# Order of the sign and the high word in an on-chip float64 to float32 conversion

## The chip, the cores and the metric

The kernel runs on one core of a Trainium2 chip. The metric is the device time of one execution in microseconds (us). Times of several runs are told as their median.

## What is computed

Attention for 4 batches of 12 heads (448 rows of 64) with RMS-normalised queries and keys, then two feed-forward blocks on the 1792 rows of 768 features:

```python
q_n, k_n = rmsnorm(q, g_q), rmsnorm(k, g_k)
attn = softmax(q_n @ k_n.T / sqrt(64))
x = heads_joined(attn @ v)
h = x @ w_in                               # 768 -> 2048
x = maximum(0.01 * h, h) @ w_out           # 2048 -> 768
h = (x @ w1) * (x @ w2) @ w3               # 768 -> 1024 -> 1024
out = (h @ w_out2).astype(float32)         # 1024 -> 768
```

All inputs of the attention are float32. The weights of the two blocks come as float64 (each was a float32 array multiplied by a float64 scalar), so the kernel gets them as pairs of 32-bit words and makes float32 of them on the chip.

## The kernel before

The program is laid out in three parts. `attention_steps` (lines 403 to 422) walks the 48 heads; for each head it emits the values of the head two before, four transposes of the probabilities of the head before, four score blocks of this head and its loads. Between these steps a generator of matrix products is advanced: first `combine_weights` (lines 564 to 591), which multiplies w3 by the last weight matrix once, then `first_mlp` and `second_mlp` (lines 630 to 686) for the first two batches, first for batch 0 alone ("early", weights of two groups), then the rest. When the heads are done, `last_pair` (lines 923 to 975) does the last two batches; it reads weights that were kept in DRAM as float32.

Each product is three matmuls for each block of 128 rows, on a high and a low part of weights and data (`group`, lines 544 to 561). After each three matmuls `group` calls `pump` (lines 529 to 535), which takes one piece of the generator `Weights.work` (lines 517 to 527) as long as fewer than two tiles are ready beyond those taken. `take` (lines 537 to 542) draws all pieces that are still missing when a tile is needed. Pieces are emitted with a priority that lets a planner place them up to 100 places earlier. The planner orders the instructions of every engine by priority and by when it reckons them ready, and gives out the buffers of the pools.

A wide weight tile (128 partitions, 768 or 512 columns, two words each) is loaded to `w64` (pool `cv`, two buffers, L459). `to_float32` (lines 461 to 486) makes float32 of it in three pieces, in a result tile `raw` (pool `wp`, three buffers):

- ScalarE takes the high word as a float and scales it by 2^-112 into `raw` (L477, called the high pass here).
- POOL makes the sign: it multiplies the high word by 0, in place, so that only its sign bit stays (L478).
- VectorE shifts `raw` left by 3 and joins the sign by "or" (L480, the join).
- ScalarE scales the low word to an integer by 2^-29, in place (L483, the low pass).
- VectorE adds the low word to the joined one as integers (L485, the add).

`split` (lines 488 to 515) then stores `raw` to DRAM if it is wanted again (L502), copies it to a rounded high part `wh` on ScalarE (L510) and subtracts that to get the low part `wl`, mostly on POOL (L203 by the helper `subtract`). There are 80 wide tiles: 8 of the last matrix, 16 of w3, 16 of w_in, 24 of w_out, 16 of w1 and w2. Kept tiles come as finished parts.

On the same engines run the attention's steps: VectorE turns the scores into p with a row minimum (L287), ScalarE takes the exponential (L296), ScalarE and VectorE copy the transposed p into two parts (L101, L203), POOL splits queries and values (`copy` L105, `subtract` L203).

Of the kernel before, what the change touches and what calls it, by code (L numbers as in the profile page):

```python
# [8 lines left out]
F32 = mybir.dt.float32  # L9
F32R = mybir.dt.float32r  # L10
U32 = mybir.dt.uint32
AF = mybir.ActivationFunctionType
ALU = mybir.AluOpType
# [35 lines left out]
def attention_then_moe(  # L49
# [22 lines left out]
    nc = tc.nc  # L72
# [352 lines left out]
    class Weights:  # L425
# [35 lines left out]
        def to_float32(self, t):  # L461

            m = self.size(t)  # L470
            self.raw[t] = wp.tile([P, WT], F32, tag="raw", name="raw")
            words = self.words.pop(t)
            low, high = words[:, :m, 0], words[:, :m, 1]
            out = self.raw[t][:, :m]
            top = out.bitcast(U32)
            signed = high.bitcast(F32)
            nc.scalar.activation(out, signed, AF.Copy, scale=2.0**-112)  # L477
            nc.gpsimd.tensor_scalar(signed, signed, 0.0, 1.0, op0=ALU.mult, op1=ALU.mult)  # L478
            yield
            nc.vector.scalar_tensor_tensor(  # L480
                top, top, 3, high, op0=ALU.logical_shift_left, op1=ALU.bitwise_or
            )
            nc.scalar.activation(low, low, AF.Copy, scale=2.0**-29)  # L483
            yield
            nc.vector.tensor_tensor(top, top, low, op=ALU.add)  # L485
            yield
# [648 lines left out]
```

## Time and profile before

| | us |
|---|---|
| median of 3 runs | 1273.02 |
| lowest and highest | 1272.32 and 1289.95 |
| the profiled execution's own time | 1278.26 |
| its span, first to last instruction | 1276.5 |
| TensorE (PE) busy in the span | 1171.5 |
| VectorE (DVE) busy | 817.2 |
| ScalarE (ACT) busy | 689.7 |
| POOL (GpSimd) busy | 496.0 |

All durations come from the one profiled execution. In the rows, PE is TensorE's matmul, PEld its weight load, DVE VectorE, ACT ScalarE, POOL GpSimd, SP the engine that issues the DMAs; `w<-w` is a tile of words, and `raw` the result tile. "L480" is line 480 of the kernel. Idle time of an engine is put down to what released the next instruction, behind "<-".

### The profile page before, as it was taken

Reading aid. Unit: us, or ns where it says so; the run is one execution under the profiler, and the core shown is the slowest. Engines: PE = TensorE matmul, PEld = TensorE weight load, DVE = VectorE, ACT = ScalarE, POOL = GpSimd, SP = SyncE. Lnnn points to the kernel's source line nnn. Section 1 sums busy time; section 2 is a strip of 40 time slices with the busy share of each in tenths; the row PEclk is TensorE's granted clock in tenths of the full one; section 3 lists DMA queues with packets and bytes.
Section 4 is the critical chain, followed back from the end, with each engine's and each line's share of the span. In section 5 each row is a group of like instructions: output and inputs, shape, how many; then the busy total and the mean of one; then the engine's idle time right before and its main releaser. Section 6 shows DMA issues by size and latency. Waiting matters only on the chain.

```text
span 1276.5 us, 17374 instructions
## 1 busy us (share of the span) xinstructions
PE 1171.5 (92%) x5816; PEld 1016.1 (80%) x5816; DVE 817.2 (64%) x1461; ACT 689.7 (54%) x1365; POOL 496.0 (39%) x470
## 2 busy tenths in 40 slices
PE   2879888898789999988989999999999999899998
PEld 1447587786668899877778899998999999699997
DVE  5986775879987465774775455358446464964553
ACT  5666666787667456545655566435442434443431
POOL 5565646777756256656766435420000000000000
PEclk9979999999889999999989999999999999899999
DMA  7767656899799955563555234135212020211212
GB/s 220 201 202 208 172 134 200 280 301 294 241 310 283 264 172 161 160 183 114 160 173 165 77 109 172 52 120 160 67 44 78 27 83 25 75 50 62 63 42 95
DMA packets 105609, 191.48 MB, mean 150 GB/s; under 512 B 23376, under 2 KB 62256, under 8 KB 105520
## 3 DMA queue, kind: packets, MB, share of 16 engines
q1 hardware_dynamic: 105520, 190.37, 49.6%
q8 instruction: 46, 0.75, 0.3%
q14 instruction: 43, 0.35, 0.1%
HBM read 136.74 MB, written 43.03 MB: 141 GB/s over the span
## 4 chain that ended last, share of the span: by engine, by line
PE 59%; DVE 14%; DMA 12%; issue 6%; POOL 5%; ACT 2%; SPq 1%; POOLq 0%; DVEq 0%; ACTq 0%
PE ps_mm L552 21%; PE ps_o L552 12%; PE ps_b L552 9%; PE ps_c L552 4%; PE pt L327 3%; PE po L381 3%; DVE raw L480 3%; PE ps_a L552 2%; PE pw L552 2%; DVE raw L485 2%; DMA w<-w 1%; PE ps L283 1%; DVE p L287 1%; PE ps L284 1%; DMA w<-w_last 1%
## 5 line engine op out<-in xcount | busy, mean ns | idle before, releaser
L203 POOL TENSOR_TENSOR wl<-raw,wh 128x512 fp32r<-128x512 f32 (+1 forms) x76 | 124.6, 1641 | 103.0 <-ACT wh L510 99.0
L296 ACT ACTIVATE p<-p,low 112x448 f32<-112x448 f32 x192 | 127.1, 663 | 55.3 <-DVE p L287 54.9
L203 DVE TENSOR_TENSOR ptl<-pt,pth 112x448 fp32r<-112x448 f32 x160 | 96.8, 617 | 80.2 <-ACT pth L101 78.0
L287 DVE TENSOR_SCALAR_CACHE_REDUCE p<-ps,rs 112x448 f32<-112x448 f32 x192 | 125.0, 676 | 35.2 <-PE pt L327 19.4
L552 PE MATMUL ps_mm<-xh,wh 128*128 128x448 f32 x384 | 142.8, 372 | 3.5 <-DMA wh<-kept_first_mlp_h 3.3
L552 PE MATMUL ps_mm<-xh,wl 128*128 128x448 f32 x384 | 142.5, 372 | 0.3 <-POOL wl L203 0.3
L552 PE MATMUL ps_mm<-xl,wh 128*128 128x448 f32 x384 | 142.7, 372 | 0.0
L327 PE MATMUL pt<-ident,p 112*112 112x112 f32 x768 | 115.2, 271 | 29.2 <-DVE ptl L203 20.5
L327 PEld LDWEIGHTS pt<-ident,p 112*112 112x112 f32 x768 | 88.3, 139 | 65.1 <-DVE ptl L203 28.4
L480 DVE SCALAR_TENSOR_TENSOR raw<-raw,w 128x768 uint32<-128x768 uint32 (+1 forms) x80 | 89.8, 1122 | 69.4 <-POOL w L478 69.2
L101 ACT ACTIVATE pth<-pt 112x448 fp32r<-112x448 f32 (+1 forms) x176 | 91.6, 534 | 49.5 <-PE pt L327 40.0
L552 PE MATMUL ps_mm<-gh,wh 128*128 128x448 f32 x288 | 107.5, 376 | 4.5 <-DVE acc L628 1.9
L283 PE MATMUL ps<-ks,qh 128*112 128x448 f32 x192 | 78.7, 413 | 32.0 <-DVE p L287 20.4
L552 PE MATMUL ps_mm<-gl,wh 128*128 128x448 f32 x288 | 106.8, 372 | 0.1
L552 PE MATMUL ps_mm<-gh,wl 128*128 128x448 f32 x288 | 106.7, 373 | 0.0
L552 PE MATMUL ps_o<-gl,wh 128*128 128x448 f32 x288 | 104.9, 365 | 0.0
L483 ACT ACTIVATE w<-w 128x768 uint32<-128x768 uint32 (+1 forms) x80 | 63.0, 788 | 74.0 <-DMA w<-w_out 25.5
L552 PE MATMUL ps_o<-gh,wl 128*128 128x448 f32 x288 | 102.5, 365 | 0.0
L552 PE MATMUL ps_o<-gh,wh 128*128 128x448 f32 x288 | 99.2, 365 | 0.8 <-DVE s L965 0.8
L477 ACT ACTIVATE raw<-w 128x768 f32<-128x768 f32 (+1 forms) x80 | 62.9, 787 | 61.5 <-POOL wl L203 22.4
L478 POOL TENSOR_SCALAR w<-w 128x768 f32<-128x768 f32 (+1 forms) x80 | 66.9, 836 | 69.3 <-ACT raw L477 59.1
L485 DVE CUSTOM_DVE_ANT_0 raw<-w,raw 128x1536 uint16<-128x1536 uint16 (+1 forms) x80 | 89.7, 1122 | 1.6
(140 smaller groups left out, 2926.7 us busy)
## 6 DMA issues: line engine op xcount, KB each, us to landing
w<-w_in SPq DMA_DIRECT2D x16, 768.0 KB, 6.2
w<-w_out SPq DMA_DIRECT2D x24, 512.0 KB, 5.3
w<-w SPq DMA_DIRECT2D x16, 768.0 KB, 4.9
qk_sb<-qk SPq DMA_DIRECT2D x48, 224.0 KB, 4.3
qt_sb<-qt SPq DMA_DIRECT2D x96, 112.0 KB, 3.6
w<-w3t SPq DMA_DIRECT2D x16, 512.0 KB, 4.8
w<-w_last SPq DMA_DIRECT2D x8, 768.0 KB, 7.1
kept_first_mlp<-raw SPq DMA_DIRECT2D x16, 384.0 KB, 4.1
```

Of the source, the lines that this page charges most:

```text
L101: nc.scalar.activation(out, x, AF.Copy)
L203: e.tensor_tensor(out, x, y.bitcast(F32), op=ALU.subtract)
L283: nc.tensor.matmul(ps, h["qh"][:, q], h["ks"], start=True, stop=False)
L287: nc.vector.tensor_scalar(p, ps, h["scale"][:, c : c + 1], None, op0=ALU.mult, op1=ALU.min, accum_out=low,)
L296: exps[i] = nc.scalar.activation(p, p, AF.Exp, bias=low, scale=-1.0, accum_out=h["sum"][:, c : c + 1])
L327: nc.tensor.transpose(pt[:, c * CP : (c + 1) * CP], h["p"][c][:, kc * CP : (kc + 1) * CP], ident[:CP, :CP],)
L477: nc.scalar.activation(out, signed, AF.Copy, scale=2.0**-112)
L478: nc.gpsimd.tensor_scalar(signed, signed, 0.0, 1.0, op0=ALU.mult, op1=ALU.mult)
L480: nc.vector.scalar_tensor_tensor(top, top, 3, high, op0=ALU.logical_shift_left, op1=ALU.bitwise_or)
L483: nc.scalar.activation(low, low, AF.Copy, scale=2.0**-29)
L485: nc.vector.tensor_tensor(top, top, low, op=ALU.add)
L552: nc.tensor.matmul(ps[:, :n], a, x, start=begin, stop=end, skip_group_check=on)
```

## The change

POOL makes the sign first, and writes it into the result tile. ScalarE scales the low word in the same piece. In a second piece ScalarE scales the high word in place. In a third piece VectorE shifts the high word, joins it with the sign and writes the result tile. The add is a fourth piece.

```diff
@@ -473,14 +473,15 @@
             low, high = words[:, :m, 0], words[:, :m, 1]
             out = self.raw[t][:, :m]
             top = out.bitcast(U32)
-            signed = high.bitcast(F32)
-            nc.scalar.activation(out, signed, AF.Copy, scale=2.0**-112)
-            nc.gpsimd.tensor_scalar(signed, signed, 0.0, 1.0, op0=ALU.mult, op1=ALU.mult)
+            h = high.bitcast(F32)
+            nc.gpsimd.tensor_scalar(out, h, 0.0, 1.0, op0=ALU.mult, op1=ALU.mult)
+            nc.scalar.activation(low, low, AF.Copy, scale=2.0**-29)
+            yield
+            nc.scalar.activation(h, h, AF.Copy, scale=2.0**-112)
             yield
             nc.vector.scalar_tensor_tensor(
-                top, top, 3, high, op0=ALU.logical_shift_left, op1=ALU.bitwise_or
+                top, high, 3, top, op0=ALU.logical_shift_left, op1=ALU.bitwise_or
             )
-            nc.scalar.activation(low, low, AF.Copy, scale=2.0**-29)
             yield
             nc.vector.tensor_tensor(top, top, low, op=ALU.add)
             yield
```

## Rows read from the trace of the kernel before

**Rows 1.** The page: the chain that ended last, share of the span by engine.

```profile
PE 59%; DVE 14%; DMA 12%; issue 6%; POOL 5%; ACT 2%; SPq 1%; POOLq 0%; DVEq 0%; ACTq 0%
```

**Rows 2.** Windows: length, PE, PEld, DVE, ACT, POOL busy us, granted clock, DMA share, GB/s.

```profile
0.00:100.00 100.00, 62.24 (x225) 37.67 (x226) 78.08 (x153) 62.81 (x120) 60.01 (x58) 0.90 0.73 208
100.00:700.00 600.00, 543.00 (x2798) 464.60 (x2797) 425.75 (x775) 378.59 (x794) 368.59 (x355) 0.97 0.70 210
700.00:850.00 150.00, 149.88 (x789) 136.38 (x789) 68.59 (x130) 78.69 (x156) 64.21 (x57) 1.00 0.30 97
850.00:1276.50 426.50, 416.42 (x2009) 377.41 (x2007) 244.73 (x404) 169.58 (x297) 3.19 (x3) 0.99 0.23 71
```

**Rows 3.** The chain by line, shares of the stretches 135:250, 250:400 and 520:700.

```profile
by line: issue 17.8%; DMA w<-w_in 12.6%; DMA w<-w3t 6.9%; PE pw L552 5.1%; POOL wl L203 5.1%; PE po L381 4.0%; DVE raw L485 3.7%; POOL w L478 3.5%; POOL ql L203 3.4%; POOL qh L105 3.2%; DMA kt_sb<-kt 2.9%; PE pt L327 2.7%; DMA wc<-wo 2.6%; 
...
by line: PE ps_mm L552 11.2%; DVE raw L480 9.1%; DVE p L287 6.0%; issue 5.8%; DVE ptl L203 5.4%; DMA rk<-rs 4.6%; DMA rk_sb<-rk 4.5%; DMA wh<-kept_first_mlp_h 4.4%; DVE raw L485 4.1%; DMA v_sb<-v 4.1%; DMA w<-w_out 3.5%; PE po L381 3.3%; DM
...
by line: issue 18.4%; PE ps_mm L552 18.0%; DMA w<-w 9.6%; DVE raw L480 6.3%; POOL w L478 3.9%; POOL wl L203 3.4%; DVE raw L485 3.4%; PE pt L327 3.3%; DMA w<-w_out 2.8%; POOL ql L203 2.6%; DMA rd<-r 2.2%; POOL qh L105 2.0%; DVE acc L628 1.8%
```

**Rows 4.** Groups by line: a weight load; busy, mean ns | idle before, by releaser.

```profile
L552 PEld LDWEIGHTS ps_mm<-gh,wh 128*128 128x128 f32 x288 | 54.8, 191 | 10.9 <-DMA wh<-kept_first_mlp_h 2.1 <-ACT w L483 1.7 <-ACT wh L510 1.3
```

**Rows 5.** Groups by line and shape: the conversion's instructions.

```profile
L480 DVE SCALAR_TENSOR_TENSOR raw<-raw,w 128x768 uint32<-128x768 uint32 x40 | 52.4, 1310 | 38.7 <-POOL w L478 38.6
...
L478 POOL TENSOR_SCALAR w<-w 128x768 f32<-128x768 f32 x40 | 38.0, 949 | 39.5 <-ACT raw L477 35.4 <-DMA qt_sb<-qt 3.1 <-DVE ss L155 1.0
L480 DVE SCALAR_TENSOR_TENSOR raw<-raw,w 128x512 uint32<-128x512 uint32 x40 | 37.4, 935 | 30.8 <-POOL w L478 30.6
L483 ACT ACTIVATE w<-w 128x768 uint32<-128x768 uint32 x40 | 36.3, 907 | 39.0 <-DMA w<-w 24.3 <-DMA w<-w_in 14.6
L477 ACT ACTIVATE raw<-w 128x768 f32<-128x768 f32 x40 | 36.3, 907 | 28.9 <-POOL wl L203 15.1 <-DMA w<-w_last 11.1 <-POOL ql L203 1.6
...
L478 POOL TENSOR_SCALAR w<-w 128x512 f32<-128x512 f32 x40 | 29.0, 724 | 29.8 <-ACT raw L477 23.7 <-DMA ks<-kh 3.1 <-DMA rb<-rd 2.7
L483 ACT ACTIVATE w<-w 128x512 uint32<-128x512 uint32 x40 | 26.8, 669 | 34.9 <-DMA w<-w_out 25.5 <-DMA w<-w3t 6.3 <-DVE rs L164 2.3
L477 ACT ACTIVATE raw<-w 128x512 f32<-128x512 f32 x40 | 26.7, 667 | 32.6 <-DMA w<-w3t 17.3 <-POOL wl L203 7.4 <-DMA w<-w_out 7.0
```

**Rows 6.** Timeline (start, length, instruction, [idle before]) at 588, 591 and 664 us.

```profile
588.04 0.67 ACT L483 ACTIVATE w<-w 128x512 uint32<-128x512 uint32 x1 [3.82 <-DMA w<-w_out]
...
591.07 0.69 DVE L480 SCALAR_TENSOR_TENSOR raw<-raw,w 128x512 uint32<-128x512 uint32 x1 [3.15 <-POOL w L478]
...
663.76 0.95 DVE L480 SCALAR_TENSOR_TENSOR raw<-raw,w 128x768 uint32<-128x768 uint32 x1
```

**Rows 7.** Waits: who waited for whom, us in total, times, longest.

```profile
DVE raw L480 <- POOL w L478: 69.2, 38, 6.5
POOL w L478 <- ACT raw L477: 59.1, 31, 7.0
...
ACT raw L477 <- POOL wl L203: 22.4, 22, 2.4
```

**Rows 8.** Timeline of VectorE and POOL at 320 and 652 us.

```profile
320.25 4.88 DVE L480 SCALAR_TENSOR_TENSOR raw<-raw,w 128x512 uint32<-128x512 uint32 x1
...
320.47 0.57 POOL L105 TENSOR_SCALAR qh<-qt_sb 128x448 fp32r<-128x448 f32 x1
...
652.04 6.52 DVE L480 SCALAR_TENSOR_TENSOR raw<-raw,w 128x768 uint32<-128x768 uint32 x1 [0.90 <-POOL w L478]
...
651.10 0.91 POOL L478 TENSOR_SCALAR w<-w 128x768 f32<-128x768 f32 x1
651.95 1.17 POOL L392 TENSOR_TENSOR x<-x,rb 128x448 f32<-128x448 f32 x1
...
656.61 1.15 POOL L203 TENSOR_TENSOR xl<-acc,xh 128x448 fp32r<-128x448 f32 x1
```

**Rows 9.** Windows: the stretch from 651 to 660 us, columns as in rows 2.

```profile
651.00:660.00 9.00, 4.23 (x21) 3.61 (x20) 8.10 (x7) 2.83 (x6) 6.75 (x7) 0.84 0.36 103
```

## Prediction

> **What bounds the kernel now.** I read the page first. TensorE is busy for 1171.5 of 1276.5 us, 92%, and holds 59% of the chain that ended last; VectorE holds 14%, the DMAs 12%, POOL 5%, ScalarE 2% [rows 1]. An average like that hides stages, so I then cut the span where the program changes its work [rows 2]. From 850 us on, the conversion does not run at all (POOL is busy for 3.19 us there), and TensorE is busy for 416 of 426.5 us: a third of the time that the change cannot touch. From 700 to 850 us TensorE is busy for 149.88 of 150 us: there conversions run, but nothing they do can be seen. What is left is 0 to 700 us, where TensorE is idle for 37.8 us of the first 100 and 57.0 us of the next 600. The first 100 us are the start, where loads set the pace. So some 57 us, 4.5% of the span, are all that any change to the conversion could win after the start, and only the part that the conversion causes can be won.
>
> How large is that part? The chain cut by stage says it [rows 3]. From 250 to 400 us the join (VectorE, L480) holds 9.1% of 150 us = 13.7 us and the add (L485) 6.2 us. From 520 to 700 us the join holds 11.3 us, POOL's sign (L478) 7.0 us and the add 6.1 us. From 135 to 250 us the sign holds 4.0 us and the add 4.3 us. The steps of the conversion lie on the path because they stand in the queues of VectorE and POOL ahead of the attention's work, hardly because TensorE needs the weights: in the group of weight loads that shows it most, they stood 1.3 us for a finished part (L510) in 288 loads [rows 4].
>
> **The change part by part.**
>
> *Work.* Each of the 80 wide tiles keeps the same five instructions: two on ScalarE, one on POOL, two on VectorE. Forty have 768 columns, forty 512. POOL's sign took 949 and 724 ns, ScalarE's two passes 907 and 669 ns each, the join 1310 and 935 ns [rows 5]. What differs is where results land: the sign now writes a packed tile instead of every second word, ScalarE's high pass the reverse. ScalarE already does both forms, L477 into a packed tile and L483 in place, at 907 ns each for 768 columns [rows 5], so its change costs 0. For POOL no row shows the sign with a packed output; its nearest rows are the in-place sign itself, 0.91 us for 768 columns, and a copy from packed to packed (L105), 0.57 us for 448 [rows 8], which in proportion is 0.98 us for 768. I take 0, between -0.07 and +0.07 us (the distance of these rows), at most 6 us of POOL time over 80, beside 231 us of POOL idle between 100 and 700 us [rows 2]: nothing on the path. The join swaps its two inputs (which one has a stride); 0 too. No moved step issues a DMA. The load of the tile after next (L459, on SP) comes one piece later in program order, and still waits for the add of the tile whose buffer it takes, which is no later by the step chain below.
>
> *The chain of a tile.* Before: high pass (ScalarE 0.91) then sign (POOL 0.90) then join, then add. After: sign, then high pass, then join, then add. The two first hops change places, so a join is ready 0.9 + 0.9 us after the tile's words and its result tile are there, in either order. No latency is won.
>
> *Waits that go.* POOL's sign now waits for ScalarE's high pass: 59.1 us in 31 waits. ScalarE's high pass waits for POOL to free the result tile: 22.4 us in 22 waits [rows 7]. Both go, the first since POOL goes first, the second since the tile's earlier reader (L203) and its new first writer are on one engine.
>
> *Waits that come.* The high pass waits for the sign, and the join for the high pass instead of for the sign. The join's wait is now 69.2 us in 38 waits [rows 7]. ScalarE stands behind POOL at one place of each tile today (the freeing of the result tile) and at one after (the sign): the same lag, 0.9 us later. So I value ScalarE's new wait like the one that goes, 22 us, at a net of 0. Its bounds: it is gone altogether, which on the chain is at most the 7.0 us that the sign holds in its worst stage [rows 3]; or it takes over all that POOL waits for ScalarE today, 59.1 us, for which see the second rival. Behind the high pass on ScalarE stand the attention's exponentials (L296) and copies (L101), for which VectorE and TensorE wait; behind the join on VectorE stands p (L287).
>
> *POOL's freed time.* The 59 us of standing at the sign were idle time of an engine that nobody but the join waits for: of that I give 3 us to the path, between 0 and 11 us (the sign's 4.0 and 7.0 us on the chain [rows 3]). It is not more, because much of that waiting was for loads. In front of the conversions, ScalarE stood 24.3 + 14.6 + 25.5 + 6.3 us at the low pass and 11.1 + 17.3 + 7.0 us at the high pass for a tile's own load [rows 5]. A sign that goes first stands for the same load, on POOL. Where a low pass of the next tile stands for its load ahead of this tile's high pass, as at 588.04 us (3.82 us of waiting, with the join then 3.15 us late at 591.07) [rows 6], it stands there after the change too.
>
> *Held joins.* A join of 768 columns takes 0.95 us undisturbed, one of 512 columns 0.69 [rows 6]; the rows of the group say 1310 and 935 ns [rows 5]. So 40 x 0.36 + 40 x 0.245 = 24 us are extra, most of it in a few places. The worst: the join starts at 652.04, just behind its sign (651.10 + 0.91), and lasts 6.52 us, until POOL has ended a run of five instructions (651.95 to 656.61 + 1.15 = 657.76); TensorE was busy for 4.23 us of the 9 from 651 to 660 [rows 8, 9]. After the change such a join starts a high pass later, while the run of POOL goes on, and would end when the run ends: 0.9 us less of holding, 0.9 us more of waiting. So 0 for this term, between -12 and +12 us (half of the 24 either way, since the joins only meet other runs).
>
> The Trainium skill, page "SBUF — State Buffer", section "SBUF: two separate sides", says that VectorE with two inputs from SBUF and POOL share a port pair as an exclusive lock, which whoever starts first has for its whole instruction. The row agrees that the join is shut out, but it was shut out for a run of five instructions, not for one. By the rule alone, the join would lose only the rest of one instruction, and a start 0.9 us later would win about 12 us over all joins; by the row the term is 0.
>
> *One piece more.* A tile is converted in pieces, one for each step of three matmuls: six from now on, five before (three of conversion, split and load). In the early group (one batch) a w_out tile has only four steps. Counted through the code, the reserve between the split and the use falls there to 0 or 1 step, and for eight of the twenty tiles two pieces are left to the moment of use, where now it is two tiles with one. The planner pulls conversions ahead by 100 places, and the wait for finished parts is 1.3 us [rows 4], so I take 0; the upper bound is the third rival.
>
> *Sum.* 0 + 0 - 3 + 0 + 0 = -3 us. Against the profiled execution's own 1278.26 us that is 1275.3; that execution stood 5.2 us above the median of the runs, 1273.02, so a median of 1270 us.
>
> **The rivals.**
>
> *The joins come free (faster).* With a step more between sign and join, the planner may place the join where both other engines are done. Then the long holds go, (6.52 - 0.95) us at 652 and (4.88 - 0.69) us at 320 [rows 8], 9.8 us, and the sign's 11 us on the chain [rows 3]; with the rest of the 24 us it is 35. That gives 1273 - 21 to 35, say 1246 us. For it: both holds are on the path. Against: the join's place follows readiness, and the latency of a tile's chain is the same.
>
> *ScalarE stands behind POOL (slower).* If the turned order turns the 59.1 us of waiting too, ScalarE stands 59.1 - 22.4 = 37 us more than now. Between 651 and 660 us a stall of 6.5 us cost TensorE 4.8 of 9 us [rows 9], about 75% of the stall; at that rate it is +28 us, 1301 us. It decides from the point where signs queue behind POOL's runs of subtractions (five in a row, 5.8 us) and ScalarE's exponentials behind them. Against it: at the rate of the sign on the chain, 11 of 69 us, it is only +6 us.
>
> *Weights come late in the early group (slower).* Six more tiles are finished at the moment of use, each with sign, high pass, join, add, copy and subtraction of about 0.7 us each (the rows of 512 columns [rows 5]; the last two, taken alike), 4.2 us ahead of its matmul: 25 us if TensorE stands for all of it, 1298 us. Against it: the 1.3 us.
>
> *The change doesn't do what it says:* the planner orders by readiness, and the extra step moves nothing; that is no change, 1273, and inside the likeliest case.
>
> **How the numbers follow.** The likeliest case, no visible change, has 0.67, with its own range from 1258 to 1285 us: the terms' bounds of 11 and 12 us. The joins come free: 0.18. ScalarE stands: 0.10; late weights: 0.05. A measurement of this kernel tells about 2%, 25 us, from no change. So faster by more than 2% is 0.18, within 0.67, slower 0.15. The range reaches into both sides, from 1245 to 1299 us.
>
> **What would show it.** Right: the join's idle time put down to ScalarE's high pass at 50 to 80 us; POOL's sign waiting for loads, no longer for ScalarE; the high pass waiting for the sign 20 to 40 us; the join and the sign with the same mean times; 850 us onward unchanged. Wrong: joins whose mean falls to 0.95 and 0.69 us (the first rival), ScalarE's wait for the sign above 60 us with exponentials behind it (the second), or weight loads that wait for the split between 250 and 400 us (the third).

## The result, and the profile after

The changed kernel took 1288.57 us, median of 20 runs, against 1277.45 us for 20 runs of the kernel before on the same chips. The ratio is 1.0088, with a 95% interval from 1.007 to 1.0106: 0.9% slower, about 11 us. The forecast was 1270 us and "no visible change". The time lies within the range and within 2%, but on the other side of zero than the sum of -3 us.

The profiled execution took 1293.89 us, its span is 1292.1 us against 1276.5. It stands 5.3 us above the median of its runs, the one of the kernel before 0.8 us, so this pair of traces differs by some 16 us where the medians differ by 11. First the same stretches as in [rows 2], with the same columns.

```profile
0.00:100.00 100.00, 61.27 (x225) 35.50 (x226) 77.51 (x156) 63.34 (x121) 63.99 (x59) 0.94 0.75 210
100.00:700.00 600.00, 538.33 (x2719) 458.07 (x2718) 420.70 (x758) 370.59 (x776) 354.25 (x344) 0.95 0.68 204
700.00:850.00 150.00, 148.48 (x788) 134.29 (x787) 71.58 (x139) 83.92 (x166) 66.60 (x61) 1.00 0.35 110
850.00:1292.10 442.10, 432.62 (x2089) 392.49 (x2087) 248.31 (x410) 174.47 (x305) 7.92 (x6) 0.99 0.23 72
```

Read the counts of matmuls first. At 100 us both kernels have issued 225. Between 100 and 700 us the changed one issues 2719 where it was 2798: 79 fewer. From 850 us on it has 2089 to do instead of 2009, at the same mean (432.62 / 2089 = 207 ns, 416.42 / 2009 = 207 ns). So the last stage lost nothing by itself; it does work that the stage from 100 to 700 us left over.

The same rows split what those 600 us lost. TensorE was idle for 61.7 us of them instead of 57.0, 4.7 us more. A matmul took 198.0 ns of busy time (538.33 / 2719) instead of 194.1 (543.00 / 2798), which over 2719 makes 10.6 us, and the granted clock, a mean over the time at its two levels (1 at 2.4 GHz, 0.5 at 1.2 GHz), was 0.95 instead of 0.97. So in this pair of traces less than a third of the loss is added idle time of TensorE; the rest are matmuls that took longer, with more of the time at the lower level. No run here separates the two.

Where in those 600 us? The end of the n-th matmul can be read from the timeline of TensorE in both traces; the difference is the lag of the changed kernel.

```
matmul number      400    600    800   1000   1200   1600   2400   3200   5000
before ends at   136.0  180.8  223.6  265.2  308.6  401.1  560.5  734.6 1095.2 us
after is later by  4.2    3.2    2.7   14.0   12.6   12.7   20.4   14.8   16.4 us
```

Eleven of the some 16 us come between the 800th and the 1000th matmul, 224 to 279 us. The same stretch in windows, the kernel before first, then the changed one.

```profile
200.00:285.00 85.00, 77.23 (x410) 69.23 (x409) 62.27 (x106) 61.95 (x130) 60.36 (x57) 0.96 0.84 267
```

```profile
200.00:285.00 85.00, 68.53 (x339) 59.95 (x338) 60.22 (x96) 50.95 (x108) 44.92 (x46) 0.88 0.69 211
```

Here 71 of the 79 matmuls are lost. TensorE, ScalarE and POOL are all less busy, the DMAs move 211 GB/s where they moved 267, and the granted clock is 0.88 where it was 0.96. No engine became the bound: all of them wait for one another. TensorE itself waits for p, which VectorE makes for the attention (L287), 11.0 us in these 85 where it was 0.5; the kernel before first, then the changed one.

```profile
L283 PE MATMUL ps<-ks,qh 128*112 128x448 f32 x22 | 8.5, 388 | 0.5 <-DVE p L287 0.5
```

```profile
L283 PE MATMUL ps<-ks,qh 128*112 128x448 f32 x20 | 8.9, 445 | 11.1 <-DVE p L287 11.0
```

The chain by line for 195 to 305 us of the changed kernel says what stood in front.

```profile
by line: DMA w<-w_in 17.9%; DVE raw L482 16.2%; PE ps_mm L553 12.0%; issue 9.8%; ACT p L296 6.0%; DMA rd<-r 5.7%; DVE raw L486 4.7%; ACT w L480 3.4%; ACT pth L101 3.3%; ACT w L478 3.0%; ACT wh L511 2.4%; DVE p L287 1.8%; ACT t L101 1.7%; PE
```

Loads of w_in hold 19.7 us of the 110 and the join 17.8 us. The timeline shows both at the first tile of w_in. In the kernel before, its low pass starts at 207.26, the sign at 209.37, the join at 210.30, and the load that needs the tile's buffer goes out at 214.76:

```profile
207.26 0.88 ACT L483 ACTIVATE w<-w 128x768 uint32<-128x768 uint32 x1 [3.20 <-DMA w<-w_in]
...
209.37 0.89 POOL L478 TENSOR_SCALAR w<-w 128x768 f32<-128x768 f32 x1 [2.87 <-ACT raw L477]
...
210.30 1.13 DVE L480 SCALAR_TENSOR_TENSOR raw<-raw,w 128x768 uint32<-128x768 uint32 x1 [3.14 <-POOL w L478]
...
214.76 0.42 SPq L459 DMA_DIRECT2D w<-w_in  x1
```

In the changed kernel the low pass starts at 208.07, 0.8 us later. But on POOL the sign stands behind a subtraction for which ScalarE makes the rounded part only at 218.51, and starts 11.2 us later than before; its join then meets a run of POOL instructions, and the load goes out at 232.93 instead of 214.76:

```profile
208.07 0.91 ACT L478 ACTIVATE w<-w 128x768 uint32<-128x768 uint32 x1 [1.80 <-DMA w<-w_in]
...
218.51 0.62 ACT L511 ACTIVATE wh<-raw 128x512 fp32r<-128x512 f32 x1
...
219.21 1.29 POOL L203 TENSOR_TENSOR wl<-raw,wh 128x512 fp32r<-128x512 f32 x1 [9.10 <-ACT wh L511]
220.59 0.89 POOL L477 TENSOR_SCALAR raw<-w 128x768 f32<-128x768 f32 x1
...
222.25 0.93 ACT L480 ACTIVATE w<-w 128x768 f32<-128x768 f32 x1
...
223.21 6.22 DVE L482 SCALAR_TENSOR_TENSOR raw<-w,raw 128x768 uint32<-128x768 uint32 x1 [0.33 <-ACT w L480]
...
232.93 0.37 SPq L459 DMA_DIRECT2D w<-w_in  x1
```

That rounded part belongs to a tile three earlier, whose copy the planner had put at 203.44 us in the kernel before. The change does not touch copies (L511) or subtractions (L203); what moved is their place in the queues.

The conversion's own groups of the changed kernel, by line and shape, which answer to [rows 5]:

```profile
L482 DVE SCALAR_TENSOR_TENSOR raw<-w,raw 128x768 uint32<-128x768 uint32 x40 | 51.6, 1290 | 33.1 <-ACT w L480 32.8
...
L482 DVE SCALAR_TENSOR_TENSOR raw<-w,raw 128x512 uint32<-128x512 uint32 x40 | 40.7, 1018 | 27.4 <-ACT w L480 27.4
L477 POOL TENSOR_SCALAR raw<-w 128x768 f32<-128x768 f32 x40 | 38.8, 969 | 29.1 <-DMA w<-w_last 8.4 <-DVE wl L203 7.5 <-DMA w<-w_in 5.3
...
L480 ACT ACTIVATE w<-w 128x768 f32<-128x768 f32 x40 | 36.1, 903 | 13.4 <-POOL raw L477 13.2
...
L477 POOL TENSOR_SCALAR raw<-w 128x512 f32<-128x512 f32 x40 | 30.2, 754 | 12.3 <-DMA w<-w3t 6.3 <-DMA w<-w_out 3.3 <-DMA qk_sb<-qk 1.1
```

And its waits, which answer to [rows 7]:

```profile
POOL wl L203 <- ACT wh L511: 130.6, 40, 11.7
...
DVE raw L482 <- ACT w L480: 60.1, 34, 7.7
...
ACT w L480 <- POOL raw L477: 19.4, 19, 2.7
```

The work per instruction is that of before, and the waits that the change itself makes came out nearly as forecast; that of POOL's sign for ScalarE is gone. What did not stay is the first of these rows: POOL's subtraction waited 130.6 us for the copy on ScalarE, where it was 99.0 us. The change does not edit that pair.

### The profile page after: what moved, and what is told of

Read it like the earlier page. It is cut to its first block, busy times and chain, and to the rows that moved or that the text cites. A ratio compares the mean times of both kernels' runs of the same rounds, so it can differ in the third digit from the quotient of the medians.

```text
span 1292.1 us, 17300 instructions
## 1 busy us (share of the span) xinstructions
PE 1180.7 (91%) x5816; PEld 1020.4 (79%) x5816; DVE 818.1 (63%) x1461; ACT 692.3 (54%) x1365; POOL 492.8 (38%) x470
## 4 chain that ended last, share of the span: by engine, by line
PE 48%; DMA 21%; DVE 15%; ACT 7%; issue 5%; POOL 2%; SPq 2%; ACTq 0%; POOLq 0%; DVEq 0%
PE ps_mm L553 14%; PE ps_o L553 12%; PE ps_b L553 9%; PE ps_c L553 4%; DMA w<-w_in 4%; DMA w<-w 3%; DVE raw L482 3%; DVE raw L486 3%; DMA rd<-r 2%; PE ps_a L553 2%; DVE p L287 2%; PE pt L327 2%; DMA w<-w_out 2%; PE po L381 2%; ACT p L296 2%
## 5 line engine op out<-in xcount | busy, mean ns | idle before, releaser
L203 POOL TENSOR_TENSOR wl<-raw,wh 128x512 fp32r<-128x512 f32 (+1 forms) x76 | 122.4, 1610 | 135.1 <-ACT wh L511 130.6
L203 DVE TENSOR_TENSOR ptl<-pt,pth 112x448 fp32r<-112x448 f32 x160 | 97.3, 618 | 90.3 <-ACT pth L101 79.5
L287 DVE TENSOR_SCALAR_CACHE_REDUCE p<-ps,rs 112x448 f32<-112x448 f32 x192 | 125.0, 675 | 34.9 <-PE ps L284 20.0
L482 DVE SCALAR_TENSOR_TENSOR raw<-w,raw 128x768 uint32<-128x768 uint32 (+1 forms) x80 | 92.3, 1154 | 60.6 <-ACT w L480 60.1
L477 POOL TENSOR_SCALAR raw<-w 128x768 f32<-128x768 f32 (+1 forms) x80 | 69.0, 862 | 41.4 <-DMA w<-w_last 8.4
L283 PEld LDWEIGHTS ps<-ks,qh 128*112 128x112 f32 x192 | 35.0, 185 | 61.8 <-DVE p L287 43.5
```

The costliest lines, as they stand in the source:

```text
L203: e.tensor_tensor(out, x, y.bitcast(F32), op=ALU.subtract)
L283: nc.tensor.matmul(ps, h["qh"][:, q], h["ks"], start=True, stop=False)
L287: nc.vector.tensor_scalar(p, ps, h["scale"][:, c : c + 1], None, op0=ALU.mult, op1=ALU.min, accum_out=low,)
L477: nc.gpsimd.tensor_scalar(out, h, 0.0, 1.0, op0=ALU.mult, op1=ALU.mult)
L482: nc.vector.scalar_tensor_tensor(top, high, 3, top, op0=ALU.logical_shift_left, op1=ALU.bitwise_or)
```

## The experiments

Three theories (the expectations call them P, O and N). *Piece*: the fourth piece makes the conversion late. *Turn*: the turned order of POOL and ScalarE costs. *Plan*: any edit here makes the planner order the whole kernel anew, and such orders differ by 0.5 to 1% whatever was edited. For the last speaks a comparison of the two programs: both hold the same 5784 instructions of the attention and the products on TensorE, but 1052 of them stand in another order (counted against the longest order that both have in common), and so do 262 of SP's 795 transfers and 155 of POOL's 467 instructions.

All ratios are to runs of the kernel before on the same chip.

### The piece or the turn, one at a time

The first run puts a bare piece into the kernel before, the second takes the piece out of the changed one:

```diff
             nc.gpsimd.tensor_scalar(signed, signed, 0.0, 1.0, op0=ALU.mult, op1=ALU.mult)
             yield
+            yield
             nc.vector.scalar_tensor_tensor(
```

> The kernel before with a bare extra step between the sign and the join: four conversion pieces, old order of the engines. Theory P (the fourth piece makes weights late in the early group): ratio to the kernel before 1.007 to 1.011, as the change itself. Theory O (the turned order of POOL and ScalarE costs the time): 0.998 to 1.002. Theory N (any edit makes the planner redraw the whole order of work, and the order it lands on is worth some 0.5 to 1% either way): anywhere from 0.992 to 1.010.

```diff
             nc.scalar.activation(low, low, AF.Copy, scale=2.0**-29)
-            yield
             nc.scalar.activation(h, h, AF.Copy, scale=2.0**-112)
             yield
```

> The changed kernel with the high pass in the first piece, so three conversion pieces, new order of the engines. Theory P: back to 0.998 to 1.002. Theory O: 1.007 to 1.011 still. Theory N: anywhere from 0.992 to 1.010.

Measured: 1.0111 [1.0089, 1.0134] and 1.0085 [1.0054, 1.0116]. Either edit alone costs as much as both together. Two causes of 0.9% that don't add up are hardly two causes. The first run speaks against *turn*, the second against *piece*; the first also lies just above the band of *plan*, which ended at 1.010. The wait for finished weights tells the same: the group of weight loads of [rows 4] stands 7.2 us for the copy in the changed kernel, 2.4 us in the first of these runs and 0.8 us in the second, at about the same time.

Two edits that touch neither piece nor turn:

```diff
-CONVERT_PRIORITY = 100
+CONVERT_PRIORITY = 90
```

> The kernel before with conversions pulled ahead by 90 places rather than 100, which changes no instruction and no dependence, only the planner's order. Theories P and O: 0.998 to 1.002 (the pull is hardly different). Theory N: off by 0.3 to 1% on either side.

> The changed kernel with the same pull of 90 places. Theories P and O: 1.007 to 1.011 as the change. Theory N: 0.3 to 1% away from that on either side, perhaps below 1.000.

> The kernel before with its pieces placed up to 110 places earlier instead of 100: a neutral edit that makes the planner draw the order again. If the redrawn order costs by itself and the kernel before stands at the low end of its draws, it gives 1.003 to 1.012 again. If a fourth piece or the turned steps were needed for a loss, it gives 0.997 to 1.003.

> The changed kernel with its pieces placed up to 110 places earlier. If the order decides and the change itself costs nothing, this is one more draw, anywhere from 0.997 to 1.016. If the turned steps carry a cost in every order that the planner makes freely, it is over 1.005, as two of the three free draws so far were.

Measured: the kernel before at 90 places 1.0059 [1.004, 1.0079], at 110 places 0.9989 [0.9965, 1.0013]; the changed one at 90 places 1.0158 [1.0137, 1.018], at 110 places 1.0123 [1.0095, 1.0152]. A neutral edit moves the old conversion by up to 0.6% and the changed one by up to 0.7%, almost as much as the whole change. Not all of this went the way of *plan*: the kernel before at 110 places came in the band set for the case that a fourth piece or the turned steps are needed for a loss (0.997 to 1.003), and the changed one at 110 places over the 1.005 set for turned steps that cost in every free order. The lag also arises elsewhere each time: at the 1000th matmul it is 14.0 us in the changed kernel, 0.3 us in the changed one at 90 places, which loses its 14 us by the 1400th. No single place carries it.

### The order held, the conversion exchanged

To measure the conversion without a new order, the planner's order of one kernel is written into another (`ORDERS`, one queue for each engine) as bare edges, from each instruction to the next on its engine. They make no engine wait for another. Only the 80 high passes must move, to the nearest place where the exchanged conversion can have them (on ScalarE's queue, in the median, two places later in the first run and three earlier in the second).

```diff
+        for packed in ORDERS.values():
...
+            for one, next_one in zip(queue, queue[1:]):
+                tc.add_manual_dep(next_one, one.name, rule, reason="order")
```

> The changed conversion (POOL's sign first, high pass in place after it) held to the very order of work that the planner made for the kernel before, on every engine, by order-only edges; of some 9500 instructions only ScalarE's 80 high passes move, to just behind the place where the sign ended in the trace of before. Theory N (the redrawn order costs the 0.9%): 0.997 to 1.003. Theory O (the turned order of POOL and ScalarE costs it): 1.006 to 1.011.

> The conversion of before (high pass first, sign in place) held to the order of work that the planner made for the changed kernel; only the 80 high passes move, to 0.9 us ahead of where the sign started in the trace of after. Theory N: 1.006 to 1.012. Theory O: 0.997 to 1.003.

Measured: the changed conversion in the order of the kernel before, 1.002 [0.9995, 1.0046]; the old conversion in the order of the changed kernel, 1.0118 [1.0087, 1.0149]. This is what *plan* forecast: the loss stays with the order when the conversion is taken out of it. In the stretch of the loss the columns go with the order too, for the old conversion in the new order and then the changed one in the old order:

```profile
200.00:285.00 85.00, 71.92 (x364) 63.68 (x363) 56.78 (x98) 54.58 (x114) 49.95 (x50) 0.90 0.69 215
```

```profile
200.00:285.00 85.00, 75.92 (x409) 67.65 (x408) 59.68 (x104) 59.89 (x126) 58.73 (x57) 0.96 0.82 253
```

364 and 409 matmuls, against 339 in the changed kernel and 410 in the one before. The run of the changed conversion in the old order also has longer waits. Its rows in the view of waits (lines are higher here: L488 is the sign, L492 the high pass, L495 the join):

```profile
DVE raw L495 <- ACT w L492: 100.3, 47, 6.2
...
ACT w L492 <- POOL raw L488: 45.9, 36, 3.5
```

The join's wait is 31 us longer than the 69.2 us of [rows 7] and ScalarE stands 45.9 us for the sign, over twice as long as the 19.4 us in the changed kernel. These totals can't be set against the 0.2%: the profiled execution took 1287.10 us, the slowest of this kernel's twelve (median 1278.89), and 8.8 us more than the profiled one of the kernel before.

### Is it the one place at 208 us?

The order of the changed kernel is held; a fourth result buffer (the pool's default is three) lets the sign of the first two w_in tiles go where their words have landed, and with it their high pass, join, add and the loads behind them. The second run is the control, with the buffer and nothing moved. The buffer's edit is made at each place where a result tile is taken; one of the three:

```diff
-            self.raw[t] = wp.tile([P, WT], F32, tag="raw", name="raw")
+            self.raw[t] = wp.tile([P, WT], F32, tag="raw", name="raw", bufs=4)
```

> The planner's order of the changed kernel, held on every engine, with two edits: a fourth result buffer, and the sign, high pass, join, add of the first two tiles of w_in and the loads behind them moved up to where their words had landed (for the first of them from 220.6 to about 208 us, its load from 232.9 to about 213 us). If the loss of 0.9% comes from that one place, where the changed kernel fell 12 to 14 us behind between 200 and 280 us, the time is at most 1.004 of before, and the lag at the 1000th TensorE instruction is under 5 us. If that place is only where a loss shows that the whole redrawn order carries, it stays near 1.009, and the lag comes back by the 1200th instruction.

> The control: the planner's order of the changed kernel, held on every engine, with the fourth result buffer alone and nothing moved. The buffer takes away a wait of POOL's sign for a result tile, but in this order the sign still stands behind the same POOL and ScalarE work. If order is what holds the first tile of w_in, the time stays at 1.006 to 1.012 and the first w_in sign stays near 220 us; if the buffer held it, the time falls to about 1.003 and the sign starts near 209 us.

Measured: 1.0057 [1.0029, 1.0085] with the tiles moved, 1.0082 [1.0055, 1.0109] for the control. From the two timelines, first the sign and the load behind it with the tiles moved, then the same two in the control:

```profile
208.65 0.88 POOL L488 TENSOR_SCALAR raw<-w 128x768 f32<-128x768 f32 x1
...
214.75 0.35 SPq L470 DMA_DIRECT2D w<-w_in  x1
```

```profile
221.77 0.91 POOL L488 TENSOR_SCALAR raw<-w 128x768 f32<-128x768 f32 x1
...
231.39 0.37 SPq L470 DMA_DIRECT2D w<-w_in  x1
```

The move did what it should: the sign is 13 us earlier, the load goes out at 214.75, as in the kernel before. But the 1000th matmul is only 1.3 us earlier (a lag of 9.9 against 11.2 us), and the gain of 0.25% lies within the two intervals. My reading of the timeline, that this place makes the loss, missed its lag (under 5 us). The time, 1.0057, lies between the 1.004 of that reading and the 1.009 of the other, and its interval holds 1.004. So this place does not make the whole lag; what share of the loss it has is not shown.

TensorE's rows show one reason. Of the 11.0 us for which it stands for p in the changed kernel, 2.53 us end at 231.21, behind the held join and its add; 5.11 us end at 268.63, behind another join and add that VectorE took 6.2 us for. With the tiles moved the first of these is smaller, and the second is there still, at 264.38. The changed kernel first, then the run with the tiles moved:

```profile
231.21 0.46 PE L283 MATMUL ps<-ks,qh 128*112 128x448 f32 x1 [2.53 <-DVE p L287]
...
268.63 0.71 PE L283 MATMUL ps<-ks,qh 128*112 128x448 f32 x1 [5.11 <-DVE p L287]
```

```profile
237.32 0.46 PE L285 MATMUL ps<-ks,qh 128*112 128x448 f32 x1 [1.47 <-DVE p L289]
...
264.38 0.72 PE L285 MATMUL ps<-ks,qh 128*112 128x448 f32 x1 [5.10 <-DVE p L289]
```

The control sets a limit to such readings. It has the order of the changed kernel, instruction for instruction, but not this wait of 5 us, and its lag is 11.2 us at the 1000th and 6.0 us at the 1600th matmul, where the changed kernel's is 14.0 and 12.7. A lag read from one execution can be off by several us without any change of order.

### Is the planner's order worse for the changed conversion as a rule?

At 90, 100 and 110 places the changed conversion was 1.0, 0.9 and 1.3% slower than the old one. So the fourth buffer was given to both, with the order left to the planner, at the same three settings.

> The changed kernel with a fourth result buffer, order left to the planner. Another draw: by the theory that the order decides, anywhere from 0.995 to 1.015, and not tied to the buffer. By the theory that the sign's wait for a result tile costs the 0.9%, at or under 1.002 and the first w_in sign within 2 us of its words.

> The kernel before with a fourth result buffer, order left to the planner: the other half of the run that brought the changed kernel to 0.9985. If the fourth buffer gives something by itself, whatever the conversion, it is at most 0.995 and a version that beats both. If that run was a draw, this is another one, 0.995 to 1.012, with no tie to the buffer.

> Changed conversion, four result buffers, pieces up to 90 places earlier, order free. If the fourth buffer is what ends the planner's worse order: within 0.5% of the old conversion with the same settings. If the pair at 100 places was chance: about 1% slower than it, as with three buffers.

> Old conversion, four result buffers, 90 places: the other half of the pair. Both theories: 0.997 to 1.007, as the old conversion's four draws with its own pieces so far.

> Changed conversion, four result buffers, 110 places, order free. If the fourth buffer is what ends the planner's worse order: within 0.5% of the old conversion with the same settings. If chance: about 1% slower than it.

> Old conversion, four result buffers, 110 places: the other half of the pair. Both theories: 0.997 to 1.007.

| buffers, places | old conversion | changed conversion | changed - old |
|---|---|---|---|
| 3, 90 | 1.0059 | 1.0158 | +1.0% |
| 3, 100 | 1 | 1.0088 | +0.9% |
| 3, 110 | 0.9989 | 1.0123 | +1.3% |
| 4, 90 | 0.9916 [0.9885, 0.9946] | 1.0032 [1.0002, 1.0062] | +1.2% |
| 4, 100 | 1.0012 [0.9988, 1.0035] | 0.9985 [0.9961, 1.0008] | -0.3% |
| 4, 110 | 0.9993 [0.9967, 1.0019] | 1.0054 [1.0029, 1.008] | +0.6% |

Two things follow. Settings that have nothing to do with the change move the same conversion from 0.9916 to 1.0059 (old) and from 0.9985 to 1.0158 (changed). And within that spread the changed one is slower in five of six pairs, by 0.8% in the mean. The fourth buffer does not end that (+1.2, -0.3, +0.6). The first run with it, 0.9985, lay in the bands of both theories; the pairs decide: the theory that the lack of a result tile makes the order worse is not borne out, though with it the changed conversion is faster than without in each of its three settings, by 1.0% in the mean. With the order held the buffer gave nothing that shows (1.0082 [1.0055, 1.0109], the control above, against 1.0088), so that gain too comes by way of the planner. Two forecasts missed: the old conversion at 90 places lies below its band (0.997 to 1.007), and the +0.6% at 110 places lies between the two that were set (within 0.5%, about 1%).

One of these, the old conversion with four buffers at 90 places, beats both kernels: 1268.24 us, 0.8% under the kernel before. It is one draw of an order, not the worth of a buffer: the same buffer at 100 and 110 places gives 1.0012 and 0.9993.

### The exchange again, on the fastest order

> The planner's order of the old conversion with four result buffers and 90 places (0.9916), held on every engine, with the changed conversion in it: only the 80 high passes move. If the plan carries the loss, 0.990 to 0.997. If the turned steps cost it, about 1.003, as the freely planned changed kernel with these settings.

> The planner's order of the changed conversion with four result buffers and 90 places (1.0032), held on every engine, with the old conversion in it: again only the 80 high passes move. If the plan carries the loss, 1.000 to 1.008. If the turned steps cost it, about 0.992.

Measured: 0.9999 [0.998, 1.0018] and 1.0141 [1.0113, 1.0169]. Both miss: the first lies between the band of *plan* (0.990 to 0.997) and the 1.003 of turned steps that cost, the second is above the band of *plan* (1.000 to 1.008) and still farther from the 0.992 of the other. With the first exchange they make a table; the rows are orders, the columns conversions.

| order of work made for | holding the old one | holding the changed one |
|---|---|---|
| the kernel before | 1 | 1.002 |
| the changed kernel | 1.0118 | 1.0088 |
| the old one, 4 buffers, 90 places | 0.9916 | 0.9999 |
| the changed one, 4 buffers, 90 places | 1.0141 | 1.0032 |

Down a column, only the order differs: the orders made for the changed conversion are slower by 1.2 and 2.3% with the old one, by 0.7 and 0.3% with the changed one. Along a row, only the conversion differs: changed against old is +0.2, -0.3, +0.8 and -1.1%. Those four have both signs and a mean of -0.1%: the turned order of steps is not slower by itself. What they show is fit. In every row the conversion that the order was made for is the faster one, clearly in the last two rows, within the intervals in the first two. The view of waits gives a mark on each of the last two orders, but not the same one. On the fastest order, first with its own conversion, then with the changed one:

```profile
DVE raw L480 <- POOL w L478: 59.1, 38, 5.0
```

```profile
DVE raw L495 <- ACT w L492: 91.1, 51, 5.8
...
ACT w L492 <- POOL raw L488: 35.7, 32, 3.5
```

Here the join waits 32 us more. On the order of the changed conversion with four buffers and 90 places, first with its own conversion, then with the old one:

```profile
DVE raw L482 <- ACT w L480: 51.2, 38, 5.9
```

```profile
POOL w L490 <- ACT raw L488: 98.3, 54, 6.0
...
DVE raw L494 <- POOL w L490: 27.1, 15, 3.1
```

Here the join of the misfit waits 24 us less, POOL's sign stands 98.3 us for the high pass, and the time is longer, by 1.1% in the medians and by 0.3% between the two profiled executions that these rows are from. So the misfit is measured, but no single wait explains it.

## Why the prediction was wrong in sign

*The failed step is "One piece more", and with it the sentence that the planner orders by readiness and the extra step moves nothing.* I costed each moved instruction against an order of all others that I took as fixed. It is not: the edit changed the place of 1052 instructions on TensorE. That was worth +0.7% with the changed conversion held fixed (1.0088 against 1.002, each within 0.2 to 0.3%), some 9 of the 11 us, and no term of the sum stood for it. I counted reserves of pieces instead, and put the term's upper bound at late weights; the weights were later (7.2 us for the copy against 1.3), but the run without the extra piece, with 0.8 us, was as slow. So it is not the piece as such: either half of the edit made the planner draw another order.

*The base.* The forecast of 1270 us stood on the median of three runs, 1273.02; twenty runs gave 1277.45. That is 4.4 of the 18.6 us between 1270 and 1288.57. And 2% was taken for the least that a measurement tells; these runs told 0.9%, with 0.2% either way.

*The sum itself, -3 us with bounds of some 12,* measured +0.2% [-0.05, +0.46], +2.6 us, with the order of the kernel before held. Right as "nothing visible" on that order; the -3 us for POOL's freed time are not seen there. On the fastest order the same exchange costs 0.8%, some 10 us, within the bounds but visible, and on the two orders made for the changed conversion it gives -0.3 and -1.1%.

*Work: 0.* Right. The sign took 969 and 754 ns (949 and 724 before), within the 0.07 us given; ScalarE's high pass 903 and 666 ns. The join takes 92.3 us over all 80 against 89.8.

*Waits.* The join's wait for the high pass, 60.1 us, is in the band of 50 to 80. The high pass waits 19.4 us for the sign, as valued (like the 22.4 us that went), just under the band of 20 to 40. POOL's sign waits for loads, no longer for ScalarE; once it also stands 7.5 us for a subtraction on VectorE (L203), which the argument that the reader of the result tile and its new writer are on one engine left out.

*Held joins: 0.* Right as a sum, though other joins are held: that at 223.21 lasts 6.22 us, until 0.8 us after POOL has ended a run of instructions. By the timeline of POOL in the changed kernel it ran five of them back to back from 223.17 us, to 227.75 + 0.87 = 228.62:

```profile
223.17 1.14 POOL L392 TENSOR_TENSOR x<-x,rb 128x448 f32<-128x448 f32 x1
224.28 1.14 POOL L203 TENSOR_TENSOR ql<-qt_sb,qh 128x448 fp32r<-128x448 f32 x1
225.39 1.28 POOL L203 TENSOR_TENSOR wl<-raw,wh 128x512 fp32r<-128x512 f32 x1
226.64 1.14 POOL L203 TENSOR_TENSOR xl<-x,xh 128x448 fp32r<-128x448 f32 x1
227.75 0.87 POOL L477 TENSOR_SCALAR raw<-w 128x768 f32<-128x768 f32 x1
```

The Trainium skill, "SBUF — State Buffer", section "SBUF: two separate sides", gives the port pair to whoever starts first for its whole instruction. This trace, like [rows 8], has VectorE's join out for the run. The 12 us by the rule alone did not come.

*The rivals.* "ScalarE stands behind POOL" fell: its sign was a wait above 60 us, and ScalarE stood 19.4 us for the sign in the changed kernel and at most 45.9 us in any run of the changed conversion. "The joins come free" fell: their means are 1290 and 1018 ns, not 950 and 690. "Weights come late" showed its mark at a quarter of its size, and is not needed for the loss. "The change doesn't do what it says" was the nearest in thought, since it looked at the planner, and farthest off in what it made of it.

*850 us on unchanged* held: 207 ns a matmul in both.

*What stays open.* Why the planner's order is slower for the changed conversion in five of six pairs. The rows give one mark: POOL's subtraction waits 117 to 138 us for the copy in all freely ordered runs of the changed one (with its four pieces), 91 to 102 us in those of the old one with three, and 119 and 121 us in the two runs with half of the edit each. But the changed one with four buffers at 100 places has 128.4 us and is at 0.9985, so the mark alone makes no time. With six pairs that spread by up to 1.7% within a column, a mean of 0.8% could still be partly chance.

## What to carry to other kernels

Where a planner orders the work, an edit has two costs: that of its own instructions, and that of the new order of all others. Bound the second first, by two or three neutral edits (here -0.1 to +0.7% around either kernel for the places, +1.1% for a bare piece, -1.0% for a fourth buffer under the changed conversion at 100 places), and don't read an effect of that size as the edit's. To split the two, hold each order and exchange the edit in it, in both directions: one exchange alone also measures how badly an edit fits an order that was made without it.

## What the runs showed that I had not expected

A stall that leads the chain need not be worth its length: two loads moved up by 14 to 17 us (from 231.39 and 242.18 to 214.75 and 227.91) gave TensorE 1.3 us at the 1000th matmul, less than two executions of one order differ by. And the total of one wait does not rank two kernels: on one and the same order the old conversion's join waited 27.1 us and the changed one's 51.2 us, and the old one was the slower.
